# u of batch 2 transposed by TensorE instead of the DMA crossbar, and a new issue order for a fused linear-attention and MLP-mixer kernel

## The chip, the cores and the metric

The kernel runs on one core of a Trainium2 chip. That core has five engines with a queue of instructions each: PE (TensorE, matrix products; its weight loads are shown apart as PEld), DVE (VectorE), ACT (ScalarE), POOL (GpSimd) and SP (SyncE, which here only issues DMA transfers). An engine works through its queue in order, and an instruction that waits for another engine holds up all that stand behind it. The metric is the device time of one execution in microseconds (us). A program reads "faster" or "slower" here only against the same kernel before the change.

## The reference

Four batches, eight heads, 768 positions, head width 48. First a gated linear attention: per head a 48x48 state is decayed by alpha and gets k times v added at each position, and y is q times the state. Then an MLP mixer on x, which is y with the heads side by side (768 positions by 384 columns): one part mixes along the positions (768 to 256 to 768), one along the columns (384 to 1536 to 384).

```python
for t in range(S):
    state = alpha[:, :, t, :, None] * state + np.einsum('bhd,bhe->bhde', k[:, :, t], v[:, :, t])
    y[:, :, t] = np.einsum('bhd,bhde->bhe', q[:, :, t], state)
...
xt = x.transpose(0, 2, 1)
h = np.maximum(xt @ w_tok1, 0.0) @ w_tok2
u = x + h.transpose(0, 2, 1)
h2 = np.maximum(u @ w_ch1, 0.0) @ w_ch2
return (u + h2).astype(np.float32)
```

Inputs and output are float32; the kernel computes most products in bf16.

## The kernel before

The attention is computed in 12 blocks n = 0 to 11: three blocks of 256 positions for each of the four batches, and in a block two halves of 128. Instead of the recurrence the kernel forms logarithms of alpha, sums them along the positions with a triangular product, takes E (the exponential of the sum) and IE (its inverse), scales q by E and k by IE, and then works with plain products and a triangular mask. The mixer of batch b starts when the six x tiles of its three blocks are there, so the attention of later batches is computed between the mixer's products of earlier ones.

There is no scheduler in the kernel. A function `build` makes a list of named steps, each with its tiles and with what has to be done before it. One table of text, `ORDER` (lines 376 to 432), gives the order in which all steps are issued, and with the last letter of each word the engine: t PE, s ACT, v DVE, g POOL, y SP. A second table, `BUFS`, gives the buffer that each new tile takes. So the place of a step among the steps of its engine is what the table says; the waits follow from the tiles. A third rule (`shared`, line 693) makes certain steps on DVE and POOL wait for each other where the table changes from one of the two engines to the other.

The names that matter here, with n a block, b a batch, i one of six row tiles, and half or hf one of two:

- `ld_at`, `ld_kt`, `ld_qt`, `ld_vt` n: loads of alpha, k, q, v (line 548), all issued by SP; `ldw_...`: loads of weights, `cw_...`: their casts to bf16. All of these use 22 buffers named `in`, which the output tiles share.
- `P`, `ln`, `lnP`, `cum`/`cumw`, `E`, `IE` n: the sums and exponentials; `k0a`, `q0r`: products that correct k and q for alternate positions; `kk`, `kl` and `qq`, `ql`: k and q scaled (line 662, tiles `pkk`, `pkq`).
- The scaled k and q have to be transposed. For blocks 0 to 5 PE does it (`trk`, `trq`, line 675, and the evictions `evk`, `evq` to the tiles `tpk`, `tpq`). For blocks 6 to 11 it is done by the DMA crossbar, issued by SP (`dk`, `dq`, line 686, into `tpk`), and `pq` copies the transposed q into `tpq`.
- `G0_`, `G1_`, `mask0_`, `mask1_`: scores and their mask (line 729); `ka`, `kb`, `kc`: halves of the scaled k moved between partitions; `kc` waits for the transpose of k, since it overwrites its source; `K`: products of k and v for the state; `s`, `sa`, `sm`: state; `vb`, `vs0_`, `vs1_`: v cast and moved; `ia`, `ib`, `y0_`, `y1_`: the output products, `x0_`, `x1_`: their eviction.
- Mixer: `t1_b_m_kc` (line 815), `ht_b_m`, `t2_b_i` (line 820), `u_b_i` (line 824). Then u has to be transposed into the tile `ut`, of which there is one buffer. For batches in `UP` PE does it: `up_b_p` for p = 0 to 2 (six transposes of 128x128 each, line 831) and `ut_b_p`, its eviction by DVE or ACT (line 834). For the others the crossbar does it: `ux_b_half` (line 690), two DMAs issued by SP.
- `c1_b_mc_half` (line 839, three products each), `rt_b_mc_half` (lines 810 and 812, eviction with the maximum), `c2_b_i_q` (line 844, three products each), `o_b_i` (line 848), `st_b_i`: store (line 588), issued by SP or ACT.
- `f1_...` and `f3_...`: products of zeros that nobody reads (line 612), 11 steps at the start of the program.

The wait of a step `c1` on the transposed u differs between the two ways:

```python
preds=(uts[0:2 + half] if b in UP else [uts[half]]) + [wl[("wc1", mc // 2)]],
```

With PE, the products of half 0 wait for the first two evictions `ut` and those of half 1 for all three; with the crossbar each half waits for its own DMA.

Of the kernel before, what the change touches and what calls it, by code (L numbers as in the profile page):

```python
# [101 lines left out]
UP = (0, 1)  # L102
# [15 lines left out]
def build(g):  # L118
# [166 lines left out]
    def mixer(b):  # L285
# [27 lines left out]
        uts = []  # L313
        if b in UP:
            for p in range(3):
# [74 lines left out]
rt_0_3_1s cw_wc12g c1_0_5_0t c1_0_6_1t rt_0_6_1s c1_0_0_1t c1_0_1_1t c1_0_4_1t k0a3v kk3v kl3v trk3t kb3s IE4s  # L390
c1_0_5_1t ld_qt3y q0r3v ld_vt3y rt_0_5_0v rt_0_4_1v c1_0_9_0t rt_0_1_1s vb3s vs1_3s vs0_3s ql3g rt_0_7_0v c1_0_2_1t
rt_0_5_1v qq3g trq3t ldw_wc15y cw_wc15s c1_0_8_1t rt_0_0_1v evk3v c1_0_8_0t rt_0_8_0s evq3v rt_0_2_1s rt_0_9_0s ka3g
kc3g K3t s0_3v sa1_3v ld_at5y P5g c1_0_11_0t c1_0_4_0t rt_0_4_0s c1_0_11_1t ld_qt4y q0r4g rt_0_11_0v lnP5s G0_3t ln15s
G1_3t c1_0_10_1t rt_0_11_1s ldw_wc20y c1_0_10_0t cum5t ldw_wc21y rt_0_8_1s mask0_3v mask1_3v rt_0_10_1s c1_0_9_1t
cw_wc20s ld_kt4y ldw_wc22y rt_0_10_0s y0_3t x0_3v IE5s ib3t ldw_wc23y qq4g ql4g trq4t cw_wc21g r15s y1_3t c2_0_4_0t
c2_0_5_0t cw_wc22s c2_0_2_0t c2_0_2_1t evq4v E5s kk4g c2_0_5_1t k0a4v kl4v trk4t sm1_3v evk4v cw_wc23s rt_0_9_1s
c2_0_1_0t ka4g ldw_wc24y x1_3s ld_kt5y k0a5v kk5g kb4g c2_0_1_1t G1_4t mask1_4v cw_wc24s kc4s G0_4t mask0_4v c2_0_5_2t
c2_0_4_1t c2_0_2_2t ldw_wc25y cw_wc25s ld_vt4y vb4s vs0_4s c2_0_4_2t ld_qt5y c2_0_4_3t o_0_4v q0r5v qq5v trk5t
c2_0_1_2t vs1_4s ia4t y0_4t x0_4s t1_1_1_0t t1_1_1_1t evk5s K4t sa0_4v sm0_4g c2_0_5_3t o_0_5v trq5t sa1_4v c2_0_2_3t
o_0_2v c2_0_1_3t t1_1_1_2t ib4t y1_4t evq5s G0_5t mask0_5v ld_at6y P6g sm1_4g G1_5t mask1_5v c2_0_0_0t ld_vt5y  # L400
c2_0_0_1t ld_at7y P7g c2_0_0_2t vb5s vs0_5s kc5s K5t x1_4s c2_0_0_3t ia5t y0_5t t1_1_0_0t t1_1_0_1t c2_0_3_0t sa0_5v
sm0_5v lnP7s lnP6s ld_kt6y k0a6v t1_1_1_3t vs1_5s ib5t y1_5t ld_kt7y k0a7g x0_5s ln16s ld_at8y cum6t P8g t1_1_0_2t
t1_1_0_3t t1_1_0_4t ld_at9y o_0_1v t1_1_1_4t x1_5s t1_1_1_5t o_0_0v ht_1_1v t1_1_0_5t c2_0_3_1t cum7t P9v ld_qt6y r16s
ln17s ht_1_0s t2_1_1t u_1_1v IE6s kk6g t2_1_2t IE7s lnP8s t2_1_0t u_1_0v t2_1_3t u_1_3v ld_qt7y u_1_2v ld_kt8y
c2_0_3_2t ld_vt6y r17s t2_1_4t u_1_4v q0r6g t2_1_5t u_1_5v ld_vt7y up_1_0t up_1_1t ut_1_1v ut_1_0s cum8t E8s c2_0_3_3t
up_1_2t c1_1_0_0t E7s lnP9s dk6y c1_1_11_0t c1_1_1_0t kb6g ld_kt9y q0r7v kk7v rt_1_1_0v E6s c1_1_2_0t rt_1_2_0v
c1_1_6_0t c1_1_5_0t c1_1_9_0t dk7y ut_1_2v c1_1_2_1t rt_1_0_0v c1_1_6_1t rt_1_11_0v o_0_3v rt_1_6_0v rt_1_2_1v qq7g
ld_qt8y vb6s ka6s IE8s rt_1_5_0v qq6g c1_1_7_0t c1_1_4_0t rt_1_4_0v c1_1_3_1t ln18s r18s vs1_6s kc6s vs0_6g K6t s0_6v
rt_1_9_0v rt_1_7_0s k0a9g c2_1_1_0t c1_1_8_0t vb7s vs0_7g c1_1_1_1t sa1_6v ln19s ka7s vs1_7s rt_1_8_0s rt_1_1_1v
c1_1_3_0t rt_1_3_0v k0a8g sm1_6g rt_1_3_1s ld_at10y kk8v P10v c1_1_8_1t dq6y kc7s c1_1_0_1t c1_1_7_1t c1_1_5_1t  # L410
ld_qt10y q0r8v qq8g dq7y rt_1_8_1s c1_1_9_1t c1_1_11_1t kb7s rt_1_5_1v rt_1_7_1s rt_1_6_1s rt_1_0_1v rt_1_9_1v pq6s
c1_1_10_0t lnP10s K7t sa0_7v sm0_7g cum9t IE9s kk9g rt_1_10_0v rt_1_11_1v c1_1_10_1t rt_1_10_1v c1_1_4_1t rt_1_4_1s
c2_1_1_1t c2_1_1_2t sa1_7v sm1_7g ld_vt8y G1_6t mask1_6v G0_6t mask0_6v c2_1_3_0t c2_1_3_1t c2_1_1_3t o_1_1v E9s
# [489 lines left out]
```

## Time and profile before

| | |
|---|---|
| three runs | 162.04, 163.16, 163.5 us; median 163.16 |
| the profiled execution | 162.72 us, of which the span from first to last instruction is 161.0 |
| PE busy | 153.2 us, 95% of the span, 1583 products |
| DVE, ACT, POOL busy | 114.8, 101.7, 68.8 us |
| read from and written to HBM | 25.17 and 4.72 MB |
| granted clock of TensorE | 1.00 |

The span is what the profile explains; 1.7 us of the execution lie outside of it. PE's busy time counts overlapped products once and includes the time in which a product only drains, so it is not a measure of how much could be saved. In the rows of the profile a line of the kernel stands for all steps that use it: line 607 is a helper through which nearly all of the attention's products go, and line 706 and 707 are the copy helper on ACT and on DVE or POOL.

### The profile page before, as it was taken

What the parts mean: (1) busy time and instruction counts of PE and PEld (TensorE: products, weight loads), DVE (VectorE), ACT (ScalarE), POOL (GpSimd) and SP (SyncE); (2) the same over time, 40 slices, a digit from 0 to 9 for tenths busy, and PEclk for the clock granted to TensorE, in tenths of its full rate; (3) what the DMA queues carried; (4) which work ended last, traced back from release to release, by engine and by line L of the source; (5) the groups of instructions that cost most, each with busy time, mean ns of one, the idle gap of its engine ahead of it and who ended that gap; (6) DMA issues with size and microseconds to landing.
All of it is one profiled execution on the core that took longest, in us unless ns stands there. A gap on an engine that the chain in (4) does not pass through costs nothing.

```text
span 161.0 us, 4005 instructions
## 1 busy us (share of the span) xinstructions
PE 153.2 (95%) x1583; PEld 99.3 (62%) x1583; DVE 114.8 (71%) x208; ACT 101.7 (63%) x189; POOL 68.8 (43%) x83
## 2 busy tenths in 40 slices
PE   7988998999999999999999979999999999999992
PEld 4556865556675776766666646666666556666661
DVE  5189996878998898999999849878773632732061
ACT  3789878789997999699998863554832000455000
POOL 4013655217936265789489769991220000000000
PEclk9999999999999999999999999999999999999999
DMA  4999999996999999999999999997402370712035
GB/s 121 325 325 326 360 320 314 333 285 165 337 370 326 246 302 254 269 248 243 182 275 154 216 249 207 222 183 218 151 2 102 62 183 0 274 46 75 0 111 183
DMA packets 76322, 34.46 MB, mean 214 GB/s; under 512 B 68112, under 2 KB 76304, under 8 KB 76304
## 3 DMA queue, kind: packets, MB, share of 16 engines
q1 hardware_dynamic: 74144, 31.27, 76.1%
q10 hardware_dynamic: 2160, 2.95, 5.1%
q8 instruction: 12, 0.20, 0.5%
q14 instruction: 6, 0.05, 0.1%
HBM read 25.17 MB, written 4.72 MB: 186 GB/s over the span
## 4 chain that ended last, share of the span: by engine, by line
PE 87%; DVE 5%; ACT 4%; issue 1%; POOL 0%; DVEq 0%
PE ps L839 29%; PE ps L844 29%; PE ps L607 18%; PE ps L815 5%; PE ps L820 4%; PE ps L675 2%; ACT tpq L706 1%; DVE u L824 1%; DVE pkq L662 1%; DVE pkk L662 1%; PE ps L831 1%; ACT tpk L706 1%; DVE wc L707 1%; ACT IE L646 1%; ACT E L646 1%
## 5 line engine op out<-in xcount | busy, mean ns | idle before, releaser
L844 PE MATMUL ps<-wc,rt 128*128 128x384 bf16 (+2 forms) x300 | 52.7, 319 | 0.0
L839 PE MATMUL ps<-ut,wc 128*128 128x384 bf16 x288 | 50.7, 326 | 0.2
L810 ACT ACTIVATE rt<-ps 128x384 bf16<-128x384 f32 x51 | 23.2, 493 | 27.9 <-PE ps L839 25.2
L839 PEld LDWEIGHTS <-wc 128*128 128x128 bf16 x288 | 27.2, 98 | 17.5 <-DVE wc L707 0.5
L844 PEld LDWEIGHTS <-rt 128*128 128x128 bf16 x300 | 27.3, 98 | 16.3
L812 DVE TENSOR_SCALAR rt<-ps 128x384 bf16<-128x384 f32 x45 | 23.0, 552 | 12.1 <-PE ps L839 11.6
L729 DVE TENSOR_TENSOR gtm<-ps,mk 128x1024 bf16<-128x1024 f32 x24 | 28.5, 1219 | 2.6 <-PE ps L607 2.4
L848 DVE TENSOR_TENSOR in<-ps,u 128x384 f32<-128x384 f32 (+2 forms) x25 | 12.9, 538 | 13.5 <-PE ps L844 13.3
L662 POOL TENSOR_TENSOR pkq<-in,E 128x384 bf16<-128x384 f32 (+1 forms) x12 | 15.7, 1320 | 11.9 <-DVE in L658 5.7
L706 ACT CAST vb<-in 64x384 bf16<-64x384 f32 (+1 forms) x24 | 15.2, 632 | 2.2 <-DMA in<-in_v_dram 0.9
L824 DVE TENSOR_TENSOR u<-ps,x 128x384 bf16<-128x384 f32 x24 | 11.8, 550 | 1.8 <-PE ps L820 1.7
L662 POOL TENSOR_TENSOR pkk<-in,IE 128x768 bf16<-128x768 f32 (+1 forms) x7 | 11.1, 1584 | 3.4 <-DVE pkk L662 1.5
L781 POOL TENSOR_TENSOR ss<-tmp,E 128x384 bf16<-128x384 f32 x9 | 7.5, 833 | 9.7 <-DVE tmp L778 6.5
L706 ACT CAST x<-ps 128x384 bf16<-128x384 f32 x17 | 8.1, 484 | 4.1 <-PE ps L607 3.9
L815 PE MATMUL ps<-x,wt 128*128 128x384 bf16 x48 | 10.5, 326 | 0.0
L820 PE MATMUL ps<-ht,wt 128*128 128x384 bf16 x48 | 9.4, 325 | 0.6 <-ACT ht L810 0.6
L607 PE MATMUL ps<-zs 128*128 128x384 f32 (+1 forms) x22 | 8.5, 517 | 1.1 <-DVE zs L508 1.1
L662 DVE TENSOR_TENSOR pkk<-in,IE 128x384 bf16<-128x384 f32 (+1 forms) x10 | 6.1, 633 | 4.2 <-ACT IE L646 4.0
L707 POOL CAST vb<-in 64x384 bf16<-64x384 f32 (+1 forms) x10 | 5.6, 564 | 7.5 <-PE ps L607 7.0
L607 PE MATMUL ps<-tpq,tpk 48*64 48x128 bf16 (+1 forms) x288 | 8.1, 219 | 0.6 <-ACT tpk L706 0.4
L607 PE MATMUL ps<-vb,gtm 128*128 128x48 bf16 x192 | 8.6, 183 | 0.0
L592 POOL TENSOR_TENSOR in<-in 128x384 f32<-128x384 f32 x7 | 7.0, 1000 | 3.5 <-DMA in<-in_alpha_dram 3.5
(90 smaller groups left out, 208.6 us busy)
## 6 DMA issues: line engine op xcount, KB each, us to landing
in<-in_alpha_dram SPq DMA_DIRECT2D x12, 384.0 KB, 5.6
in<-in_k_dram SPq DMA_DIRECT2D x12, 384.0 KB, 4.9
in<-in_v_dram SPq DMA_DIRECT2D x12, 384.0 KB, 5.2
in<-in_q_dram SPq DMA_DIRECT2D x12, 384.0 KB, 4.9
in<-in_moe_w_ch_dram SPq DMA_DIRECT2D x12, 384.0 KB, 6.0
out_dram<-in ACTq DMA_DIRECT2D x15, 192.0 KB, 1.9
in<-in_moe_w_tok_dram SPq DMA_DIRECT2D x4, 384.0 KB, 6.3
out_dram<-in SPq DMA_DIRECT2D x8, 192.0 KB, 2.1
```

What stands on the lines that cost most here:

```text
L607: return self.pe.matmul(out, lhsT=lhsT, rhs=rhs, start=start, stop=stop, skip_group_check=True)
L662: self.shared(self.eng[e].tensor_tensor(self.t(dst)[:, c : c + z, :, 0:D], self.t(src)[:, :, c : c + z, :].rearrange("p h s d -> p s h d") ...
L706: return self.act.copy(d, s)
L729: self.nc.vector.tensor_tensor(self.t(gtm)[:, hf, :, :], self.pair(gp).rearrange("p a (j t) -> p (a j) t", t=128), bass.AP(tensor=m.tensor ...
L810: self.act.activation(d, s, AF.Relu)
L812: self.nc.vector.tensor_scalar_max(d, s, 0.0)
L815: self.pe.matmul(self.bank(bank)[:, 0:HD], lhsT=self.wt1[:, kc, m * 128 : m * 128 + 128], rhs=self.t(x), start=(kc == 0), stop=(kc == NS - 1))
L820: self.pe.matmul(self.bank(bank)[:, 0:HD], lhsT=self.wt2[:, kc, i * 128 : i * 128 + 128], rhs=self.t(hts[kc]), start=(kc == 0), stop=(kc = ...
L824: self.nc.vector.tensor_tensor(self.t(u)[:, i % 3], self.bank(bank)[:, 0:HD], self.t(x), ALU.add)
L839: self.pe.matmul(self.bank(bank)[:, 0:HD], lhsT=self.wc1[:, kc, mc * 128 : mc * 128 + 128], rhs=self.t(ut)[:, 3 * half : 3 * half + 3, kc, ...
L844: self.pe.matmul(self.bank(bank)[:, 0 : cz - ca], lhsT=self.t(rts[mc][0])[:, i * 128 : i * 128 + 128], rhs=self.wc2[:, mc, ca:cz], start=( ...
L848: self.nc.vector.tensor_tensor(self.row(o)[:, ca:cz], self.bank(bank)[:, 0 : cz - ca], self.t(u)[:, i % 3, ca:cz], ALU.add)
```

## The change

One constant is changed, and the two tables are replaced as a whole (their lines are not shown; a line of each stands for the rest). The number of steps goes from 946 to 950.

```diff
-UP = (0, 1)
+UP = (0, 1, 2)
...
 ORDER = """
-f1_trq1t f3_cumw1t f3_K0t ld_at0y ln0s f3_trk0t ld_at1y ln1s f3_cumw0t cumw0t IE0s cumw1t E1s IE1s Et1s Et0s ld_kt0y
...
+ld_at0y ln0s ld_at1y ln1s f1_trq1t f3_trk0t f3_trq1t f3_cumw0t cumw0t f3_cumw1t ld_qt0y f1_trq0t cumw1t E0s ld_kt0y
...
```

- Batch 2 joins `UP`. The two crossbar DMAs `ux_2_0` and `ux_2_1` go; three steps `up_2_p` with 18 transposes on PE and three evictions `ut_2_p` (two on DVE, one on ACT) come. Batch 3 stays with the crossbar.
- All steps stand in a new order, and some on another engine: 43 instead of 45 of the `rt` evictions on DVE and 53 instead of 51 on ACT; three instead of one of the `pq` on POOL; eight instead of three of the `qq` on DVE; 14 instead of 10 stores on SP. The order is said to have been worked out with the transfers that bring instructions counted as pauses, at places found by counting products; nothing of that stands in the kernel but the table itself.

Three places where the order differs. The first is DVE at the start of the program, blocks 0 to 2, behind the memsets: from the scaled q and k (line 662) to the first masks (`gtm`) and states (`ss`). The tiles: `tpk`, the transposed k; `vb`, the cast v. Before:

```order
L662 TENSOR_TENSOR pkk_97<-in_85,IE_94 128x8x48 x2
L707 CAST vb_102<-in_80 128x768
L772 TENSOR_TENSOR ss_114<-ps,E_90 128x384
L707 COPY tpk_107<-ps 128x1024
L662 TENSOR_TENSOR pkq_95<-in_68,E_90 128x8x48 x2
L662 TENSOR_TENSOR pkq_96<-in_70,E_91 128x8x48 x2
L772 TENSOR_TENSOR ss_115<-ps,E_90 128x384
L662 TENSOR_TENSOR pkk_98<-in_76,IE_93 128x8x48 x2
L729 TENSOR_TENSOR gtm_110<-ps,mk 128x1024 x2
L729 TENSOR_TENSOR gtm_111<-ps,mk 128x1024
L662 TENSOR_TENSOR pkk_99<-in_66,IE_94 128x8x48
```

And in the change:

```order
L662 TENSOR_TENSOR pkq_96<-in_84,E_90 128x8x48 x2
L662 TENSOR_TENSOR pkk_98<-in_77,IE_93 128x8x48 x2
L662 TENSOR_TENSOR pkk_97<-in_64,IE_94 128x8x48 x2
L707 COPY tpk_104<-ps 128x1024
L707 COPY tpk_106<-ps 128x1024
L729 TENSOR_TENSOR gtm_111<-ps,mk 128x1024
L772 TENSOR_TENSOR ss_116<-ps,E_90 128x384
L729 TENSOR_TENSOR gtm_111<-ps,mk 128x1024
L772 TENSOR_TENSOR ss_115<-ps,E_90 128x384
L729 TENSOR_TENSOR gtm_110<-ps,mk 128x1024
L772 TENSOR_TENSOR ss_117<-ps,E_91 128x384
L662 TENSOR_TENSOR pkk_99<-in_69,IE_94 128x8x48 x2
```

The scaled q of block 1 (`qq1`, `ql1`) and the cast `vb0` left DVE, the second transposed k (`evk1`) came to it, the first mask is the ninth instruction of this piece instead of the thirteenth (an x2 is two), and the scalings of block 2, of which one was on DVE before, are all there: two in the last row shown, `ql2` and `qq2` behind it.

The second place is SP's queue in the third quarter of the attention, from the first crossbar transpose (`dk6`) on. `tpk<-pkk` is a `dk`, `tpk<-pkq` a `dq`. Before (`dk6`, `ld_kt9`, `dk7`, `ld_qt8`, `ld_at10`, `dq6`, `ld_qt10`, `dq7`, `ld_vt8`, `ld_qt9`, `dk8`, `dq8`):

```order
L686 DMA_TRANSPOSE tpk_107<-pkk_97 128x8x128
L548 DMA in_81<-in_k_dram 128x8x96
L686 DMA_TRANSPOSE tpk_104<-pkk_98 128x8x128
L548 DMA in_82<-in_q_dram 128x8x96
L548 DMA in_74<-in_alpha_dram 128x8x96
L686 DMA_TRANSPOSE tpk_105<-pkq_96 128x8x128
L548 DMA in_83<-in_q_dram 128x8x96
L686 DMA_TRANSPOSE tpk_106<-pkq_95 128x8x128
L548 DMA in_84<-in_v_dram 128x8x96
L548 DMA in_66<-in_q_dram 128x8x96
L686 DMA_TRANSPOSE tpk_105<-pkk_99 128x8x128
L686 DMA_TRANSPOSE tpk_107<-pkq_96 128x8x128
```

And in the change (`dk6`, `dq6`, `ld_vt9`, `ld_qt8`, `ld_kt9`, `ld_qt9`, `ld_vt8`, `dk7`, `dk8`, `dq7`, `ld_at10`, `dq8`):

```order
L686 DMA_TRANSPOSE tpk_106<-pkk_99 128x8x128
L686 DMA_TRANSPOSE tpk_107<-pkq_95 128x8x128
L548 DMA in_83<-in_v_dram 128x8x96
L548 DMA in_75<-in_q_dram 128x8x96
L548 DMA in_80<-in_k_dram 128x8x96
L548 DMA in_76<-in_q_dram 128x8x96
L548 DMA in_66<-in_v_dram 128x8x96
L686 DMA_TRANSPOSE tpk_107<-pkk_98 128x8x128
L686 DMA_TRANSPOSE tpk_104<-pkk_97 128x8x128
L686 DMA_TRANSPOSE tpk_105<-pkq_96 128x8x128
L548 DMA in_85<-in_alpha_dram 128x8x96
L686 DMA_TRANSPOSE tpk_106<-pkq_95 128x8x128
```

`dq6` moved up to stand behind `dk6`; `dk7` moved down, behind five loads, and `dq7` from the eighth to the tenth of these places.

The third place is DVE around the u of batch 2 (six rows of line 824). Before:

```order
L729 TENSOR_TENSOR gtm_111<-ps,mk 128x1024
L824 TENSOR_TENSOR u_133<-ps,x_119 128x384
L824 TENSOR_TENSOR u_133<-ps,x_123 128x384
L824 TENSOR_TENSOR u_133<-ps,x_118 128x384
L729 TENSOR_TENSOR gtm_111<-ps,mk 128x1024
L707 CAST x_124<-ps 128x384
L824 TENSOR_TENSOR u_130<-ps,x_120 128x384
L824 TENSOR_TENSOR u_130<-ps,x_125 128x384
L824 TENSOR_TENSOR u_130<-ps,x_126 128x384
L729 TENSOR_TENSOR gtm_110<-ps,mk 128x1024 x2
```

And in the change:

```order
L729 TENSOR_TENSOR gtm_111<-ps,mk 128x1024 x2
L824 TENSOR_TENSOR u_132<-ps,x_124 128x384
L824 TENSOR_TENSOR u_131<-ps,x_118 128x384
L824 TENSOR_TENSOR u_131<-ps,x_122 128x384
L824 TENSOR_TENSOR u_131<-ps,x_126 128x384
L824 TENSOR_TENSOR u_132<-ps,x_119 128x384
L824 TENSOR_TENSOR u_132<-ps,x_120 128x384
L707 COPY kt_100<-pkk_97 64x8x48
L707 COPY ut_134<-ps 128x768 x2
L707 CAST x_125<-ps 128x384
```

The six u now stand together, and behind them `ka10` (`kt<-pkk`) stands ahead of the two evictions `ut_2_0` and `ut_2_2`.

130 lines of the change are left out of this document (65 added, 65 removed), and 22 rows, old and new, of the table BUFS.

## Prediction

> **What bounds the kernel now.** I read the page first, then the busy time of a long stretch, then PE's own waits, then the chain that ended last.
>
> ```profile
> span 161.0 us, 4005 instructions
> PE 153.2 (95%) x1583; PEld 99.3 (62%) x1583; DVE 114.8 (71%) x208; ACT 101.7 (63%) x189; POOL 68.8 (43%) x83
> ...
> 31.00:157.80 126.80, 125.69 (x1262) 80.93 (x1262) 91.43 (x155) 77.63 (x150) 57.69 (x60) 1.00 0.78 193
> ```
>
> The second row is the one to dwell on: from 31 us to the last product PE is busy for 125.69 of 126.80 us at full clock. Only 1.11 us of that long part is idle. So PE bounds the kernel, and what a new order could win behind 31 us is 1.1 us at most; the rest could only come from the start and from the 3.2 us behind the last product.
>
> ```profile
> PE ps L607 <- DVE zs L508: 1.1, 1, 1.1
> PE ps L607 <- POOL pkk L707: 1.1, 1, 1.1
> PE ps L820 <- ACT ht L810: 0.6, 1, 0.6
> PE ps L607 <- ACT la L601: 0.5, 1, 0.5
> ```
>
> PE's waits name nearly all of it: the start, one wait for `pkk` on POOL, and two in the first 31 us. The chain shows what that start consists of:
>
> ```profile
> 6.70 0.82 ACT IE L646
> 7.54 1.03 DVE pkk L662 x2
> ...
> 12.71 1.20 ACT tpq L706
> 13.96 1.21 ACT tpq L706
> 15.17 0.88 ACT tpk L706
> 16.10 1.87 PE ps L607 x45
> ...
> 25.67 0.50 ACT ht L810
> ...
> 30.08 0.87 DVE wc L707
> 30.99 6.02 PE ps L839 x36
> ...
> 157.56 0.33 issue
> ```
>
> Three evictions in a row on ACT (`evq0`, `evq1`, `evk1`) hold up PE until 16.1, `ht` holds it at 25.7, and the cast of a weight (`cw_wc11`) until 30.99. From there it is products to the end.
>
> **The change part by part.** *Eighteen transposes more on PE.* Their price stands in batch 1:
>
> ```profile
> 37.02 0.45 PE ps L675 x8
> ...
> 65.87 0.67 PE ps L831 x12
> ...
> L831 PE MATMUL ps<-idn,u 128*128 128x128 bf16 x36 | 2.9, 220 | 0.1
> ...
> L707 DVE COPY ut<-ps 128x768 bf16<-128x768 bf16 x4 | 2.2, 548 | 0.0
> L706 ACT COPY ut<-ps 128x768 bf16<-128x768 bf16 x2 | 1.6, 788 | 1.5 <-PE ps L831 1.5
> ```
>
> Twelve in 0.67 are 0.056 us each, so 18 cost 1.0 us, all of it on the path, since PE has no idle time to hide them: **+1.0**. The three evictions (two of 0.55 on DVE, one of 0.79 on ACT) need cover. Behind `up_2_0` PE still has `y0_9`, `up_2_2` and `c2_1_2_3` to do, 8, 6 and 3 products or 0.20 + 0.34 + 0.49 = 1.03 us by their steps in the trace; an eviction on DVE with the latency of a product (about 0.2) takes 0.75. It is covered if DVE is free then, which is a rival below.
>
> The Trainium skill (VectorE: DVE Perf Modes, The three transpose paths) gives 390 ns for a 128x128 bf16 transpose by TensorE and 1309 ns by the crossbar. If each of the 18 held PE for that long, the estimate from that page would be 7.0 us instead of 1.0. The row of twelve in 0.67 us speaks against reading the figure so: it is a latency, and the transposes overlap.
>
> *Two crossbar DMAs less.*
>
> ```profile
> DMA to landing us min/median/max: 3.3/3.4/5.8
> ```
>
> That is from issue to landing for the four `ut` DMAs, and nothing is named as waiting for them: PE had `c2_1` products and an attention block in between. Taking the first two out wins nothing on PE. If their cover had been gone it would have been up to 3.4; a gain here is excluded, because PE was not idle there.
>
> *The wait of `K9`.*
>
> ```profile
> 86.86 2.66 SPq L686 DMA_TRANSPOSE tpk<-pkk  x1
> ...
> DMA to landing us min/median/max: 3.0/4.8/6.7
> ...
> 93.69 0.50 POOL L707 COPY pkk<-pkk 64x384 bf16<-64x384 bf16 x1 [1.81 <-ACT x L706]
> ...
> 94.25 0.34 PE L607 MATMUL ps<-vb,pkk 128*128 128x96 bf16 x4 [1.06 <-POOL pkk L707]
> ```
>
> `kc9` on POOL is named as released by ACT, but by the code it waits for `dk9`, and `dk9` issued at 86.86 with the longest landing of its kind (6.7) arrives at 93.56, just ahead of 93.69. In the change `dk9` has two loads fewer in front of it and `K9` 1.9 us more PE work, so I take the wait as gone: **-1.06** (ends: 0 and -1.06).
>
> *The start.*
>
> ```profile
> 4.32 0.84 ACT L601 ACTIVATE la<-in 128x768 bf16<-128x768 f32 x1 [2.23 <-DMA in<-in_alpha_dram]
> ...
> 103.26 2.36 DVE L729 TENSOR_TENSOR gtm<-ps,mk 128x1024 bf16<-128x1024 f32 x2 [0.65 <-PE ps L607]
> ```
>
> Before, the first scores wait for `evq0` (12.71 + 1.20 = 13.9), and the first mask comes at about 14.5. In the change `E0` and `qq0`, `ql0` go first, and `evk0`, `evk1` are on DVE. With the same loads (`alpha` of blocks 0 and 1, then q, k) I add: `ln0` ends at 5.16, so the sum of block 0 starts at 5.2 and lasts 1.0; `E0` 0.82 (as `IE0`) to 7.1, two scalings 1.03 to 8.1, `trq0` to 9.1, `evq0` on ACT behind the exponentials of block 1 from 9.6 to 10.9, scores to 11.6; an estimate from these rows. From there to `ht_0_1` DVE has 6 masks at 1.17 (half of 2.36) and 12 instructions at 0.47 (two in a row take 1.03, the last of them 0.56), together 12.7, and three waits of 0.2 to 0.5 (for `K0`, `G0_1`, `y1_2`), an estimate of 1.0 in all: 25.3, against 25.5 before. So the 2.9 us won on the first mask are given back, since three scalings came from POOL to DVE. Next, `cw_wc12` on DVE stands in the place of `cw_wc11`, behind `ut_0_1`, and the second `c1` starts at 31.0 as before. But `trk3` (0.45) is then already done on PE, where it came at 36.9 before: **-0.4** (ends: -1.5, if DVE's waits fall away and the weight comes earlier; +1.0, if block 2's v comes late).
>
> *Everything else that moved.* Before, there is 0.05 us of unexplained idle time behind 31 us, so it can only get worse. Where it is tight is shown by the queue of SP:
>
> ```profile
> 5.51 2.34 SPq L548 DMA_DIRECT2D in<-in_q_dram  x2
> ...
> 80.49 2.60 SPq L686 DMA_TRANSPOSE tpk<-pkk  x1
> 83.20 1.24 SPq L686 DMA_TRANSPOSE tpk<-pkq  x1
> ...
> 85.06 0.64 PE L607 MATMUL ps<-tpq,tpk 48*64 48x128 bf16 x32
> ```
>
> Loads in a row go at 1.17 each; a transpose behind a load takes 2.6, behind a transpose 1.24. In the change five loads stand between `dq6` and `dk7`, and `dq7` is the third transpose behind them. `dq6` waits for `qq6` on DVE, which ends at about 70.4: before, 75.4 us of PE's work, by the counts of its products, were done when `G0_7` began at 85.06, so the offset is 9.7, less the 0.4 of the start; `qq6` stands at 60.1 us of work, and takes 0.96. Then 1.24 + 5 x 1.17 + 2.6 + 1.24 + 1.24 later the issue of `dq7` is done (82.6), and it lands some 2.0 to 4.2 behind that (the landing row above counts 3.0 to 6.7 from the start of an issue of 1.24 to 2.6): 84.6 to 86.8. `pq7` takes 1.35, and PE reaches `G0_7`, with 77.7 us of work ahead of it, at 77.7 + 9.3 = 87.0. So the wait lies between 0 and 1.2. A second such place follows on POOL (below). I take **+0.6** for all of these, near the lower end (ends: 0 and 3), since the loads and transposes of 65 to 111 us run at the pace of the queue either way and a wait at one place gives slack at the next. Bringing instructions, 12 transfers of 16 KB for PE, stays the same in number within one, and no wait of PE's products is put down to it; I set it at nothing.
>
> Sum against the profiled execution: 162.72 + 1.0 - 1.06 - 0.4 + 0.6 = 162.86. That execution was 0.44 below the median of the three runs; I go a third of that way up and forecast **163.0**.
>
> **The rivals.** *The transposed q and k come late (slower).* Blocks 7 to 9 depend in the change on one another: `dk9` is written into the buffer that `pq7` reads, so it can't be issued before `pq7` ends, and `dq9` stands behind it. `pq9` went to POOL, and there the work of block 10 follows in a row:
>
> ```profile
> 94.61 1.34 ACT L706 COPY tpq<-tpk 128x1024 bf16<-128x1024 bf16 x1 [0.90 <-DMA tpk<-pkq]
> ...
> 102.72 0.64 PE L607 MATMUL ps<-tpq,tpk 48*64 48x128 bf16 x32
> ...
> L707 POOL COPY tpq<-tpk 128x1024 bf16<-128x1024 bf16 x1 | 1.3, 1345 | 0.1
> L662 POOL TENSOR_TENSOR pkq<-in,E 128x768 bf16<-128x768 f32 x6 | 10.1, 1682 | 3.9 <-DVE in L658 2.0 <-DVE pkk L662 1.7
> L781 POOL TENSOR_TENSOR ss<-tmp,E 128x384 bf16<-128x384 f32 x9 | 7.5, 833 | 9.7 <-DVE tmp L778 6.5 <-ACT tpq L706 3.1
> L654 POOL TENSOR_TENSOR in<-in,in 128x384 f32<-128x384 f32 x5 | 5.0, 999 | 2.8 <-DVE in L654 2.6
> L662 POOL TENSOR_TENSOR pkk<-in,IE 128x768 bf16<-128x768 f32 x5 | 9.1, 1816 | 1.9 <-DVE in L654 0.9 <-ACT IE L641 0.8
> ```
>
> `pq9`, `qq10`, `sm1_9`, `P11`, `k0a10`, `kk10` are 1.35 + 1.68 + 0.83 + 1.0 + 1.0 + 1.82 = 7.7 us. Behind `kk10` waits `ka10` on DVE, and behind that the two evictions `ut_2_0` and `ut_2_2`, without which no `c1_2` can start. `c1_2_0_0` has 93.1 us of PE's work ahead of it; `G0_10`, with 91.1, began at 102.72 before, so without the 1.06 and the 0.4 it is due at 103.2. So `kk10` has to end by 102.2 (0.27 for `ka10`, 0.55 and the latency for the eviction) and `dq9` to land by 94.5. It landed at 94.6 before, where `pq9` was released. From there on each us of delay is a us on PE, for which nothing else stands ready. If the queue is 2 to 3 us later than I reckon, the time is 164.8 to 166.0. Against it: fewer loads lie ahead of `dk9`, and neighbouring transposes are cheap. Chance 0.28.
>
> *The start gives more (faster).* If the early mask isn't given back, because DVE's other instructions find gaps, `ht_0_0` and u come up to 1.5 earlier beyond my 0.4: 161.3 or a little below. Against it: by the counts DVE has three scalings more to do there now, and the casts of weights behind it wait for loads that land no earlier. Chance 0.10.
>
> *Each transpose holds PE for its whole latency.* By the row above a product of this form lasts 0.22 when alone; 18 in line would be 4.0, not 1.0, and the time 166.0. The page of the Trainium skill named above would make it 169.0. The row of twelve speaks against both. Chance 0.02.
>
> *The forecast*, PE full with a few small waits: 0.60.
>
> **How the numbers follow.** 1%, 1.6 us, is about what a measurement of this kernel can tell from no change. The forecast's own range is 161.8 to 164.6: inside. The late transposes and the serial ones lie beyond it above (0.30), the better start below (0.10). The range that should hold 8 in 10 takes in half of either side: 161.4 to 165.5.
>
> **What would show it.** In the profile after: `L831` with 54 products; PE busy some 1.0 us longer and its idle time behind 31 us below 1.1 us; no wait of `K9`; the first mask near 11.6 and the second `c1` still near 31. It is wrong if PE waits at `G0_7`, `G0_9` or the first `c1_2` for more than 1 us together, or if the weights' products start more than 1 us away from 31.

## The result and the profile after

| | before | after |
|---|---|---|
| median, on the same chip | 162.37 us | 163.43 us |
| lowest to highest | 161.49 to 163.5 | 162.72 to 163.85 |
| after / before | | 1.0057, 95% interval 1.0039 to 1.0076 |
| the profiled execution | 162.72 us | 162.93 us |

The change makes the kernel slower by 0.6%, about 0.9 us by the ratio and 1.06 by the two medians. (The ratios are worked out from the fast runs on each chip and can differ a little from the quotient of two medians.) The forecast was 163.0, inside 1% of no change. Against its own base, the profiled execution, it allowed the change 0.14 us; beside the median of 163.16 shown for before it was even a small gain, of 0.16. So the time was 0.43 off, but a loss of about 1 us was forecast as a draw. The two profiled executions alone, 0.2 us apart, would have confirmed the forecast: most of what follows is about why that would have been wrong.

The page of the kernel after, its first and its busy line, and the busy time from 31 us to 158 us (columns: length, then busy time and instructions of PE, PEld, DVE, ACT, POOL, then granted clock, DMA share, GB/s):

```profile
span 161.2 us, 4044 instructions
PE 154.4 (96%) x1601; PEld 100.3 (62%) x1601; DVE 119.2 (74%) x214; ACT 98.1 (61%) x184; POOL 66.7 (41%) x85
```

```profile
31.00:158.00 127.00, 126.88 (x1275) 81.76 (x1273) 95.33 (x160) 75.53 (x149) 53.33 (x59) 1.00 0.75 190
```

PE has 18 products more, and is idle for 0.12 us in 127. The bound is what it was; there is simply more in it. PE's waits in the kernel after:

```profile
PE ps L607 <- DVE zs L508: 1.1, 1, 1.1
PE ps L820 <- ACT ht L810: 0.6, 1, 0.6
PE ps L607 <- DVE gtm L729: 0.4, 1, 0.4
PE ps L675 <- DVE pkk L662: 0.3, 1, 0.3
PE ps L815 <- DVE x L707: 0.3, 1, 0.3
```

All five lie in the start. The wait for `pkk` on POOL (`K9`) is gone, as forecast. The chain that ended last, up to the row of `c1` products:

```profile
4.26 5.05 DMA in<-in_k_dram
9.40 1.03 DVE pkk L662 x2
11.09 2.14 PE ps L607 x35
...
28.81 1.20 DVE u L824 x3
30.75 0.87 DVE wc L707
31.67 5.05 PE ps L839 x30
```

The three evictions on ACT that stood in the chain of before are out of it; loads and DVE took their place, and the long row of `c1` stands in it from 31.67 on instead of 30.99.

To compare more than two executions I split each profile at one point: the first product of the second `c1` step (the 30.99 and 31.67 of the two chains), and the end of the last product. What lies behind that end is 4.81 to 4.88 us in the profiled executions of before and after, and plays no part. All figures are read or subtracted from the traces; the kernels are told of below. A wait is counted here from the moment at which the product would have followed the one before it; the rows of the profile count idle time from the end of that product, and show 0.16 to 0.19 us less for the same wait.

| kernel | second c1 at | last product ends | between | wait of PE over 0.3 us in between |
|---|---|---|---|---|
| before | 30.99 | 157.84 | 126.85 | 1.22 at `K9` |
| before, copy (b_copy) | 31.83 | 157.70 | 125.87 | none |
| before, copy (b_copy2) | 31.84 | 159.08 | 127.24 | 1.36 in block 5 (0.80 at a `c2_0`, 0.56 at `trk5`) |
| before, copy (b_copy3) | 31.93 | 158.28 | 126.35 | none |
| e3, `dk9` earlier | 31.21 | 156.87 | 125.66 | none |
| e8, `dk9` later | 31.00 | 157.26 | 126.27 | 0.61 at `c1_2_1_0` |
| e5, PE transposes in the old order | 32.30 | 159.94 | 127.63 | 0.74 at `G0_10` |
| after | 31.67 | 158.12 | 126.45 | none |
| after, copy (a_copy) | 31.52 | 157.95 | 126.43 | none |
| e6, transposes twice | 32.47 | 159.89 | 127.42 | none |
| e11, three transposes | 31.54 | 157.96 | 126.42 | three of 0.2 to 0.3, 0.76 together |

### The profile page after: what moved, and what is told of

Read it like the earlier page. It is cut to its first block, busy times and chain, and to the rows that moved or that the text cites. A ratio compares the mean times of both kernels' runs of the same rounds, so it can differ in the third digit from the quotient of the medians.

```text
span 161.2 us, 4044 instructions
## 1 busy us (share of the span) xinstructions
PE 154.4 (96%) x1601; PEld 100.3 (62%) x1601; DVE 119.2 (74%) x214; ACT 98.1 (61%) x184; POOL 66.7 (41%) x85
## 4 chain that ended last, share of the span: by engine, by line
PE 84%; DVE 6%; DMA 3%; SPq 2%; ACT 1%; issue 1%; POOL 1%; DVEq 0%; POOLq 0%
PE ps L844 29%; PE ps L839 29%; PE ps L607 14%; PE ps L815 5%; PE ps L820 4%; DMA in<-in_k_dram 3%; SPq L548 2%; DVE u L824 1%; PE ps L675 1%; PE ps L831 1%; DVE pkk L662 1%; DVE ss L772 1%; DVE pkq L662 1%; DVE wc L707 1%; POOL vb L707 1%
## 5 line engine op out<-in xcount | busy, mean ns | idle before, releaser
L844 PE MATMUL ps<-wc,rt 128*128 128x384 bf16 (+2 forms) x300 | 51.9, 320 | 0.0
L839 PE MATMUL ps<-ut,wc 128*128 128x384 bf16 x288 | 49.9, 326 | 0.1
L810 ACT ACTIVATE rt<-ps 128x384 bf16<-128x384 f32 x53 | 24.2, 492 | 22.6 <-PE ps L839 22.3
L662 POOL TENSOR_TENSOR pkk<-in,IE 128x384 bf16<-128x384 f32 (+1 forms) x8 | 11.2, 1407 | 7.6 <-DVE in L654 5.7
L707 POOL CAST vb<-in 64x384 bf16<-64x384 f32 (+1 forms) x15 | 8.5, 569 | 11.5 <-DVE pkq L662 3.7
L706 ACT CAST vb<-in 64x384 bf16<-64x384 f32 (+1 forms) x18 | 11.8, 656 | 1.6 <-DMA in<-in_v_dram 0.9
L662 POOL TENSOR_TENSOR pkq<-in,E 128x384 bf16<-128x384 f32 (+1 forms) x7 | 8.1, 1167 | 9.5 <-DMA in<-in_q_dram 7.9
L781 POOL TENSOR_TENSOR ss<-tmp,E 128x384 bf16<-128x384 f32 x8 | 6.7, 837 | 10.5 <-DVE pkq L662 8.5
L662 DVE TENSOR_TENSOR pkq<-in,E 128x384 bf16<-128x384 f32 (+1 forms) x10 | 7.4, 755 | 4.5 <-ACT E L646 3.5
L592 POOL TENSOR_TENSOR in<-in 128x384 f32<-128x384 f32 x8 | 8.0, 1003 | 0.4 <-DMA in<-in_alpha_dram 0.2
```

What stands on the lines that cost most here:

```text
L662: self.shared(self.eng[e].tensor_tensor(self.t(dst)[:, c : c + z, :, 0:D], self.t(src)[:, :, c : c + z, :].rearrange("p h s d -> p s h d") ...
L706: return self.act.copy(d, s)
L810: self.act.activation(d, s, AF.Relu)
L839: self.pe.matmul(self.bank(bank)[:, 0:HD], lhsT=self.wc1[:, kc, mc * 128 : mc * 128 + 128], rhs=self.t(ut)[:, 3 * half : 3 * half + 3, kc, ...
L844: self.pe.matmul(self.bank(bank)[:, 0 : cz - ca], lhsT=self.t(rts[mc][0])[:, i * 128 : i * 128 + 128], rhs=self.wc2[:, mc, ca:cz], start=( ...
```

## The experiments

In the diffs of this section that move a step, the table `ORDER` is written with one word on a line; `BUFS` changes with it and is not shown.

**The kernels unchanged, once more.** Two copies of before and after, and later two more of before.

> The kernel before, unchanged, for a second profile. Theory A (the wait of K9 is a fixed part of the order): PE again waits 1.0 to 1.1 us ahead of K9, and about 1.1 us of idle time behind 31 us. Theory B (the wait depends on when the crossbar transpose dk9 lands, which differs between executions): the wait ahead of K9 differs by 0.4 us or more, and the span with it.

> The changed kernel, unchanged, for a second profile; its first one was 0.5 us below its median. Theory A: the same 0.1 us of idle time behind 31 us, and a longer start. Theory B: some place of the stretch from 85 to 104 us (G0_7, G0_8, G0_9, K9 or the first c1_2) has a wait of 0.3 us or more that the first profile does not show.

> The kernel before unchanged, for one more profile of it. Of the profiles with its order in the middle so far, one (the first, with dk9 landing 6.7 us behind the start of its issue) has a wait of K9. If that wait is rare, none here, with dk9 landing 3.5 to 4.5 behind its issue; if it is there about half of the time, as likely as not.

> As the run before it: the kernel before unchanged, for one more profile of where dk9 lands, whether K9 waits, and when the second c1 begins (30.99 to 32.30 so far).

Measured 162.54 (b_copy), 162.78 (a_copy), 163.92 and 163.12 us (b_copy2, b_copy3), one execution each, beside a median of before of 162.59 and 162.24 on those chips. None of the three copies of before has the wait of `K9`. In b_copy POOL's copy `kc9` runs at 92.17 without any wait (in the first profile: at 93.69, behind a wait of 1.81), and PE has 0.55 us of idle time in 127 (0.30 of it behind its last product) instead of 1.11 in 126.8. POOL's row, and the busy time:

```profile
92.17 0.50 POOL L707 COPY pkk<-pkk 64x384 bf16<-64x384 bf16 x1
```

```profile
31.00:158.00 127.00, 126.45 (x1266) 81.17 (x1265) 92.57 (x157) 77.79 (x152) 57.80 (x60) 1.00 0.77 195
```

But b_copy2 has a loss of the same kind at another place, where only b_copy3 has a trace of it (0.27): in block 5, PE waits for a cast of a weight and for a scaled k.

```profile
53.90 0.49 PE L844 MATMUL ps<-wc,rt 128*128 128x384 bf16 x2 [0.64 <-ACT wc L706]
54.78 0.62 PE L675 MATMUL ps<-idn,pkk 128*128 128x128 bf16 x8 [0.39 <-POOL pkk L662]
```

So single waits of about 1 us come and go in before, at places that differ from one execution to the next. The two profiles of the kernel after differ by 0.02 us between the second `c1` and the end; the longer start that was expected of a_copy did not come (31.52).

**The wait of K9: dk9 issued earlier, and later.**

```diff
 ...
+dk9y
 ld_kt10y
-dk9y
 ...
```

> Before, with the crossbar transpose dk9 issued one place earlier, ahead of the load of k of block 10. Theory A (a wait of 1.06 us ahead of K9 in each execution): ratio 0.9935, and no wait at K9 in the profile. Theory B (the wait is there in some executions only, and smaller in the median): ratio 0.996 to 1.000.

Ratio to before 0.9992 (0.9955 to 1.0029), median 162.24. There is no wait of `K9` in the profile, and nothing clear is won: in us the interval reaches from -0.7 to +0.5, so that a wait of 1.06 in every execution (ratio 0.9935) is excluded. The other direction:

```diff
 ...
+dq9y
 dk9y
 ...
-dq9y
 ...
```

> The kernel before, with the transposing DMA dq9 issued ahead of dk9 instead of behind it; nothing else is moved. dk9 then lands one transpose later, at 93.4 to 94.6 us, where PE is ready for K9 at about 93. Theory B (K9 waits for dk9 alone, and what it waits goes into the time in full): a wait of K9 of 1.0 to 2.4 us in the profile, and a time 0.7 to 1.8 us above before, ratio 1.004 to 1.011. If a wait at K9 is given back later (PE has waits of 0.2 us only behind it, so there is little to give it back from), ratio at most 1.002.

Ratio 1.0004 (0.9969 to 1.004): missed. I had expected that `dk9` lands where `dq9` did. SP's queue and POOL's `kc9` in e8:

```profile
86.67 1.40 SPq L686 DMA_TRANSPOSE tpk<-pkq  x1
88.17 1.26 SPq L686 DMA_TRANSPOSE tpk<-pkk  x1
```

```profile
92.39 0.51 POOL L707 COPY pkk<-pkk 64x384 bf16<-64x384 bf16 x1 [0.96 <-DMA tpk<-pkk]
```

Though issued second, `dk9` landed at 92.27, 4.1 us behind the start of its issue, and PE, which reached `K9` at 93.0, did not wait. Behind its issue it landed 4.3 us in b_copy, 5.5 in b_copy2, 4.3 in b_copy3, 4.5 in e3, 3.2 in after, and 6.7 in the first profile of before, the one on which the prediction was built. So e8 did not make `dk9` late, and its time says nothing of what a late one costs. That the `K9` wait goes into the time in full where it occurs is not shown by these runs, since none of them made it occur.

**The price of the transposes in the old order.** Before, with batch 2 in `UP`; first with all three evictions on ACT.

```diff
-UP = (0, 1)
+UP = (0, 1, 2)
...
 c2_1_5_1t
+up_2_2t
+ut_2_2s
 ...
 c2_1_5_2t
+up_2_0t
+ut_2_0s
 c2_1_5_3t
+up_2_1t
+ut_2_1s
-ux_2_1y
 ...
-ux_2_0y
```

> Before, with batch 2 of u transposed by PE and nothing else moved: the two crossbar DMAs out, three PE steps and three evictions on ACT in. If 18 transposes cost 0.056 us each on the path: 1.0 us slower than before, ratio 1.006. If the crossbar DMAs that are gone make room in the queue that PE feels: ratio 1.000 to 1.003. If each transpose holds PE for its latency of 0.22 us: 4 us slower, ratio 1.024.

Ratio 1.0242 (1.0196 to 1.0288), which is about the 4 us that a price of 0.22 for each transpose would give. The trace says otherwise. PE's waits between 80 and 110 us in e1, and one row of its time line:

```profile
PE ps L607 <- ACT ut L706: 1.1, 2, 0.8
PE ps L607 <- ACT la L598: 0.8, 1, 0.8
```

```profile
103.25 0.33 PE L607 MATMUL ps<-la,u 128*128 128x400 bf16 x1 [0.78 <-ACT la L598]
104.00 0.50 PE L831 MATMUL ps<-idn,u 128*128 128x128 bf16 x6
104.34 0.65 PE L844 MATMUL ps<-wc,rt 128*128 128x384 bf16 x3
```

Six transposes take 0.34 us until the next step begins; but the evictions hold up ACT's logarithm for `cum11`, and PE waits. A number that agreed with a wrong theory by accident: the placing of the evictions cost more than the transposes. The second trial places them where DVE and ACT have room:

```diff
 y1_9t
+up_2_2t
 ...
 x1_9s
+ut_2_2s
 ...
 c2_1_5_2t
+up_2_0t
+ut_2_0v
 c2_1_5_3t
+up_2_1t
+ut_2_1v
 ...
```

> The kernel before, with only batch 2 transposed by PE: up_2_2 behind y1_9, up_2_0 and up_2_1 on both sides of c2_1_5_3, their evictions on ACT (ut_2_2, behind x1_9) and DVE (the two others, behind u_2_2), the two crossbar DMAs gone. Unlike the first trial of this edit, no eviction stands behind a row of ACT's logarithms, and up_2_1 writes into a PSUM bank that was read long before. Theory C (the price of the 18 transposes, 1.0 us, is what is left of the change, and the two DMAs taken out win nothing): 1.0 to 1.2 us slower than before, ratio 1.006 to 1.008, three steps of L831 of about 0.34 us each more, and at most 0.3 us of new waits near 100 to 105 us. Theory D (the transposes are hidden or nearly free, and what the change lost, it lost by its order): ratio 0.998 to 1.002. If each transpose held PE for 0.22 us: 4.0 us, ratio 1.024.

Ratio 1.0134 (1.0106 to 1.0162), 2.2 us. PE in e5, time line:

```profile
101.30 0.49 PE L831 MATMUL ps<-idn,u 128*128 128x128 bf16 x6
...
103.60 0.50 PE L831 MATMUL ps<-idn,u 128*128 128x128 bf16 x6
104.03 0.24 PE L607 MATMUL ps<-tpq,tpk 48*64 48x128 bf16 x1
104.82 0.64 PE L607 MATMUL ps<-tpq,tpk 48*64 48x128 bf16 x31 [0.55 <-DVE ut L707]
```

The second product of `G0_10` waits 0.74 us for a PSUM bank that `ut_2_1` is still reading. Between the second `c1` and the end e5 has 127.63, less that wait 126.89: 1.0 to 1.2 above the undisturbed 125.66 and 125.87. So theory C's size is met in the trace, but the time by itself is 1 us above what C allowed: 0.74 of it is the wait. The profile also began late (32.30), which a profile of one execution cannot attribute.

**The price in the new order, upward and downward.**

```diff
-                self.pe.transpose(o[:, c : c + 128], self.t(u)[:, (2 * p + q) % 3, j * 128 : j * 128 + 128], self.idn)
+                for _ in range(n):
+                    self.pe.transpose(o[:, c : c + 128], self.t(u)[:, (2 * p + q) % 3, j * 128 : j * 128 + 128], self.idn)
```

Here n is 2 for batch 2 and 1 for the others.

> The kernel after, in which each of the 18 transposes of batch 2 is issued twice into the same place (the result stays the same): 18 products more, no DMA, no eviction and no other instruction more. It measures their price by itself. Theory C: 1.0 us above the kernel after, so 1.9 to 2.1 above before, ratio 1.012 to 1.013; the three steps of up_2 take 0.67 us instead of 0.34. Theory D: within 0.3 us of the kernel after, ratio 1.005 to 1.008. At 0.22 us for each: 4.0 above after, ratio 1.030.

Ratio 1.0124 (1.0097 to 1.0152), 1.1 us above the kernel after. PE in after, and in e6:

```profile
102.14 0.83 PE L831 MATMUL ps<-idn,u 128*128 128x128 bf16 x12
102.81 0.36 PE L607 MATMUL ps<-vb,gtm 128*128 128x48 bf16 x8
103.01 0.49 PE L831 MATMUL ps<-idn,u 128*128 128x128 bf16 x6
103.34 0.65 PE L844 MATMUL ps<-wc,rt 128*128 128x384 bf16 x3
```

```profile
102.95 1.50 PE L832 MATMUL ps<-idn,u 128*128 128x128 bf16 x24
104.28 0.36 PE L607 MATMUL ps<-vb,gtm 128*128 128x48 bf16 x8
104.49 0.83 PE L832 MATMUL ps<-idn,u 128*128 128x128 bf16 x12
```

From one start to the next, 12 transposes take 0.67 and 24 take 1.33; between the second `c1` and the end e6 has 127.42 against 126.45. That is 0.97 us for 18, 0.054 each: the predicted price. Now downward, with 15 of the 18 left out:

```diff
-                self.pe.transpose(o[:, c : c + 128], self.t(u)[:, (2 * p + q) % 3, j * 128 : j * 128 + 128], self.idn)
+                if n or q + j == 0:
+                    self.pe.transpose(o[:, c : c + 128], self.t(u)[:, (2 * p + q) % 3, j * 128 : j * 128 + 128], self.idn)
...
-                  self.bank(bank).bitcast(BF16)[:, 0:768])
+                  bass.AP(tensor=z.tensor, offset=z.offset, ap=[list(z.ap[0]), [0, 6], [1, 128]]))
```

Here n is false for batch 2, and z is the first 128 columns of the bank.

> The kernel after, with 15 of the 18 transposes of batch 2 left out: each step of up_2 does its first only, and the evictions copy that one block six times over, so batch 2's result is not the reference's; order, evictions, DMAs and everything else stay. With the run that doubles them it shows whether the price is the same downwards. Theory C (all of the change's loss is the price of these products): 0.75 to 0.85 us below the kernel after, so within 0.3 of before, ratio 1.000 to 1.003. If something else of the new order (an eviction, a queue, the start) stands just behind them: less than 0.4 below after, ratio 1.003 to 1.006.

Ratio 1.0063 (1.0038 to 1.0089): no gain at all, where theory C expected 0.8; it is what was expected if something stands just behind the transposes. PE in e11 at this place, and DVE:

```profile
102.00 0.27 PE L832 MATMUL ps<-idn,u 128*128 128x128 bf16 x2
102.40 0.36 PE L607 MATMUL ps<-vb,gtm 128*128 128x48 bf16 x8
102.86 0.22 PE L832 MATMUL ps<-idn,u 128*128 128x128 bf16 x1
102.92 0.65 PE L849 MATMUL ps<-wc,rt 128*128 128x384 bf16 x3
103.62 2.12 PE L844 MATMUL ps<-ut,wc 128*128 128x384 bf16 x12
```

```profile
99.94 2.87 DVE L824 TENSOR_TENSOR u<-ps,x 128x384 bf16<-128x384 f32 x6
102.84 0.26 DVE L707 COPY kt<-pkk 64x384 bf16<-64x384 bf16 x1
103.02 1.01 DVE L707 COPY ut<-ps 128x768 bf16<-128x768 bf16 x2
```

PE has holes in front of `y0_9`, `up_2_2` and the first `c1_2`, 0.76 us together: the six u in a row on DVE, and the evictions behind them, set the pace. The busy time from 99 to 105 us, in after and in e11, says the same: DVE is full in both, and PE is full in after only because the transposes fill it.

```profile
99.00:105.00 6.00, 6.00 (x68) 4.10 (x67) 5.94 (x13) 3.38 (x7) 3.27 (x3) 1.00 1.16 257
```

```profile
99.00:105.00 6.00, 5.71 (x53) 3.40 (x52) 5.94 (x12) 3.50 (x8) 3.11 (x3) 1.00 1.01 270
```

From the second `c1` to the last product e11 takes 126.42 us and after 126.45. So theory C was too simple. In the new order PE and DVE are both full in this stretch: more products cost their full price, fewer of them win nothing.

**The order alone.** After, with the crossbar for batch 2.

```diff
-UP = (0, 1, 2)
+UP = (0, 1)
...
 u_2_1v
+ux_2_0y
 ...
 u_2_5v
+ux_2_1y
```

(The six steps `up_2` and `ut_2` are gone.)

> The kernel after in its own order, with batch 2's u transposed by the crossbar as before: up_2 and ut_2 are gone, ux_2_0 is issued behind u_2_1, and ux_2_1 behind u_2_5, ahead of dq10. It does the order alone. Theory C: 1.0 us of PE's work goes, and in its place PE waits at the first c1_2 products, since in this order only c2_1_2_2, t2_2_5, cum11, y1_9, y0_9 and c2_1_2_3 (2.0 us) stand between the last u of the first half and c1_2_0_0, against 3.4 us or more of a crossbar DMA: a wait of 1.4 to 2.0 for the first half and 0.3 to 1.0 for the second. Together 0.7 to 2.0 above the kernel after, ratio to before 1.010 to 1.019. Theory D (the order alone is what costs): 1.004 to 1.008. If the DMAs were covered: ratio 0.998 to 1.002.

Ratio 1.0413 (1.0371 to 1.0455), some 5.5 us above after: far beyond the expected 0.7 to 2.0. In e9, SP's queue, PE's time line, and the busy time in stretches:

```profile
103.07 3.31 SPq L690 DMA_TRANSPOSE ut<-u  x2
```

```profile
103.76 0.65 PE L844 MATMUL ps<-wc,rt 128*128 128x384 bf16 x3
107.69 6.58 PE L839 MATMUL ps<-ut,wc 128*128 128x384 bf16 x23 [3.28 <-DMA ut<-u]
```

```profile
103.00:108.00 5.00, 1.47 (x26) 0.76 (x22) 3.67 (x8) 2.70 (x6) 0.35 (x1) 0.83 0.83 156
108.00:113.00 5.00, 5.00 (x17) 2.37 (x16) 0.30 (x1) 0.49 (x1) 1.33 (x1) 0.50 1.03 267
```

The first DMA landed 4.6 us behind its issue instead of 3.4, so PE stood for 3.28 us; and behind that its granted clock was 0.50 for about five us, in which the steps of `c1` took 0.96 us instead of 0.49. The wait cost its length and then some 2.7 us more. The Trainium skill (TensorE: Matmul & The Clock Gate, What's actually happening) says that the clock is halved after an idle window of about 3.4 us and restored after a busy one of that length. The trace agrees in kind; here a wait of 3.28 us was enough, and the half clock lasted longer than 3.4 us. For this experiment it means that it does not measure the order alone. It does show that with the two DMAs at these places this order has no cover for them: they need PE's transposes, or other places.

**The start.** After, with three edits ahead of 32 us.

```diff
+y1_2t
 t1_0_1_2t
-y1_2t
 ...
-k0a3v
 ht_0_1v
 ...
+k0a3g
 kk3g
 ...
+c1_0_11_0t
 c1_0_5_0t
```

> The kernel after, with three edits in its start: y1_2 on PE ahead of t1_0_1_2, the scaling k0a3 on POOL ahead of kk3 instead of on DVE ahead of ht_0_1, and c1_0_11_0 (whose weight is there already) ahead of c1_0_5_0, which waits for the cast cw_wc12. If the start of the change is late by the order of DVE's and PE's own work (theory C: 0.2 to 0.3 us at x1_2 and 0.28 at the second c1), PE reaches the row of c1 products with 0.3 to 0.5 us less idle time, and all of it reaches the end: 0.3 to 0.5 below the kernel after, ratio to before 1.002 to 1.004. If the start goes at the pace of the loads, which land at the same times, nothing is won: 1.005 to 1.007.

Ratio 1.0044 (1.0022 to 1.0067), against 1.0057 for after. The intervals overlap: inconclusive, though on the side of a small gain.

The start of after, joined to the rest of before at the first `c2_0`:

```diff
-f1_trq1t
-f3_cumw1t
...
+ld_at0y
+ln0s
...
 c2_0_4_0t
 c2_0_5_0t
...
```

> The order of the kernel after on every engine and queue up to the first c2_0 (about 48 us), then that of the kernel before for all that is left; batch 2 by the crossbar, as before. It does the start's part of the change alone, trk3 and trk4 ahead of their old places included. The prediction's step (-0.4): ratio 0.996 to 0.999. If the start gains nothing in the median, since PE's late filler, the loads and DVE give back what the early mask wins: 0.999 to 1.002. If it costs (the second c1 began at 31.5 to 31.7 in the profiles of the kernel after, at 31.0 to 32.3 in those with the start of before, and the work done ahead is only 0.45): 1.002 to 1.005. At the seam a few waits of 0.2 to 0.3 us near 48 to 52 us are possible, which belong to neither order and are taken off by the trace.

Ratio 1.0355 (1.0306 to 1.0403). The seam spoiled it. The longest of PE's waits in e12:

```profile
PE ps L607 <- ACT la L598: 2.8, 1, 2.8
```

It is `cum5`, from 46.9 to 49.7 us, whose logarithm stands late in the joined order; another wait of 1.2 us follows at 62.2. The time therefore tells nothing of the start; its trace only adds one more beginning of the row of `c1` with this start, 32.58.

The last experiment came out of the rows of the first products. PE's first row, products of zeros which nobody reads, in before, in b_copy, in e5 and in after:

```profile
1.12 4.70 PE L607 MATMUL ps<-zs 128*128 128x128 f32 x10 [1.12 <-DVE zs L508]
```

```profile
1.12 5.61 PE L607 MATMUL ps<-zs 128*128 128x128 f32 x10 [1.12 <-DVE zs L508]
```

```profile
1.12 5.91 PE L607 MATMUL ps<-zs 128*128 128x128 f32 x10 [1.12 <-DVE zs L508]
```

```profile
1.12 4.04 PE L607 MATMUL ps<-zs 128*128 128x128 f32 x8 [1.12 <-DVE zs L508]
```

Before, b_copy and e5 have the same ten products there, in the same order, and they take 4.70, 5.61 or 5.91 us; `cumw0` stands behind them. In the eight profiles with this start `cumw0` begins at 5.59 to 6.83, and the second `c1` follows 25.3 to 25.9 us behind it: most of what differs between their starts is there from these first products on. So I left two of them out:

```diff
-f3_cumw0t
 cumw0t
 ...
 c1_0_0_0t
+c1_0_1_0t
 c1_0_3_0t
 ...
-c1_0_1_0t
 ...
+dk9y
 ld_kt10y
-dk9y
```

> The kernel before with three edits, none of them on batch 2: the filler products f3_cumw0 (on zeros, which no one reads) are left out ahead of cumw0, c1_0_1_0 (whose weight is there) stands ahead of c1_0_3_0, which waits for the cast cw_wc11, and dk9 is issued ahead of the load ld_kt10. In the traces so far the same ten filler products of before last 4.70 to 5.91 us, and cumw0 starts behind them at 5.66 to 6.83, though ln0 ends at 5.16. If the start of before is set by these fillers, cumw0 starts at 5.2 to 5.6, the row of c1 products begins 0.4 to 1.0 earlier, and the time is 0.4 to 1.2 below before, ratio 0.993 to 0.998. If DVE and the loads set the start at 20 to 30 us, only the 0.28 at c1_0_3_0 is won: ratio 0.998 to 1.000. If the filler is needed to bring PE up to speed, the products behind it are slower for longer: ratio 1.000 to 1.004.

Ratio 0.9979 (0.9959 to 1.0), median 161.77 against 162.24; in the profile `cumw0` begins at 5.32 and the second `c1` step at 30.71, the earliest of all. The row of `c1` itself begins at 30.23, no earlier than in the first profile of before (30.22), whose filler was short. The ratio lies on the border of two expectations, and the run does not tell the three edits apart. It is the fastest kernel of this study: it beats the kernel after, and leads before by 0.2%, an interval that just touches no difference.

## Why the prediction was right or wrong, by its steps

- **What bounds the kernel: right.** PE is full from 31 us on in both kernels.
- **Eighteen transposes, +1.0: right in size.** 0.97 by e6. The rival in which each holds PE for its latency is refuted: the rows count 0.22 us for one alone, and 12 in a row take 0.67. The Trainium skill (TensorE: Matmul & The Clock Gate, Wait — 56ns, not 53.3ns?) gives 55.6 ns from start to start for a product of 128 columns, which is what the rows show; so of its two pages it is this one, not the 390 ns of the transpose paths, that prices such a row. What the prediction did not see is e11: DVE is as full as PE there, so it is not the transposes alone that hold this stretch.
- **Two crossbar DMAs less, nothing won: right**, with a remark: e8's 0.61 us at `c1_2_1_0` is a wait for one of them, and b_copy and b_copy3 wait 0.2 us for the other, so their cover is thin in some executions.
- **The wait of K9, -1.06: this is the step that failed.** The reading of the wait was right (it is `dk9`, not ACT), and it is indeed absent after the change. For the two profiled executions the whole sum even holds: PE's last product comes 0.28 us later (158.12 against 157.84), by +0.97 for the transposes, -1.22 for `K9`, +0.23 for the start (0.68 later, less the 0.45 of `trk3`) and about +0.3 for the rest, and 0.14 was forecast. But the wait was taken as a fixed part of before. It occurs in one of the four profiles of the kernel before, and moving `dk9` forward (e3) changes the time by -0.1 us, with an interval of -0.7 to +0.5. Against the median of before the term is about -0.1, not -1.06. That the forecast's base was only 0.35 us above the median in spite of this wait comes from its start: 30.99, where three of its four profiles began their second `c1` at 31.83 to 31.93. A lucky start and an unlucky landing, and the prediction wrote off only the second.
- **The start, -0.4: mis-sized, about 0.** The first mask came at 11.81, as forecast (11.6). But `ht_0_1`, forecast for 25.3, came at 26.0: `y1_2` stands behind a product that it need not wait for, and `k0a3` (0.5 us of DVE) stands ahead of `ht_0_1`. Eight profiles with the start of before (the seven of the table above that have it, and e1 with 31.82) began the second `c1` at 31.6 on average (30.99 to 32.30), six with that of after (after, a_copy, e6, e9, e11, e12) at 32.1 (31.52 to 32.69): +0.5, against the 0.45 of `trk3`, which is done ahead. With spreads as large as these the 0 is uncertain by several tenths, and e7, which mends the two places, is inconclusive.
- **Everything else, +0.6: too much.** The waits at `G0_7` and `G0_8` are 0.15 and 0.11 us. The rival of the late q and k missed by a little: `dq9` landed at 94.10, where the prediction had put the limit at 94.5, and nothing waited.

The sum with measured terms: +0.97, -0.1, 0 and about +0.3 make about +1.2; measured were 0.9 to 1.1. As a check, take the averages of the second `c1` (31.6 and 32.1) and 4.85 behind the last product. After comes to 163.4 with its 126.4 us in between, for a median of 163.43. Before comes to 162.2 if nothing waits in between (125.7), and to 162.8 with the average of the six profiles of its order with the crossbar (126.4), for a median of 162.37.

What stays open is what a median execution of either kernel looks like, since none was profiled. The four profiles of before (162.54 to 163.92 us) all lie above its median of 162.37 (b_copy, 162.54, is level with the 162.59 of its own chip), and the two of after (162.93 and 162.78) lie below its median of 163.43; by the last products of these six (158.2 on average before, 158.0 after) the change would lose nothing. So the runs show the price of the transposes and that `K9` is no fixed term. That the start and the order come to nothing is worked out from traces with large spreads; the two experiments that were to show it by the time (e9, e12) brought waits of their own, so it is not shown by itself.

## What to carry to other kernels

A wait in one profile is a term of the sum only if it is there in a second profile of the same kernel; look at two or three before booking the gain of removing it, and look also for what was lucky in that execution. Where PE and DVE are both full in a stretch, price a change there in both directions: adding work costs in full, and removing it may win nothing as long as the other engine stays full. When a trial's time agrees with a theory, read the row it is about before believing it (e1 did so by accident).

## What the hardware showed that was not expected

- **PE's slow first microseconds are of varying length.** The same ten products of zeros took 4.63 to 5.91 us, depending on the execution: a step of two of them takes 1.28 us at first and 0.64 later, and the moment of the change differs. The column of the granted clock doesn't show it: in e5 it reads 1.00 in a stretch in which the steps still took 1.28. (The trace's own record of the clock begins only at 7.25 us in e5, and at 4.46 in before; ahead of that the column has nothing to go by.)

```profile
5.00:6.00 1.00, 1.00 (x3) 0.58 (x2) 0.00 (x0) 0.65 (x2) 0.00 (x0) 1.00 1.17 325
```

  The Trainium skill (TensorE: Matmul & The Clock Gate, What you observe) puts the doubling of the rate at about 4 us of sustained products, within 0.5 from run to run. That it varies agrees, but the 1.3 us between the shortest and the longest row is more than the 1.0 which that allows.

  These 1.3 us are as much as the whole effect of this change.
- **Behind a wait of 3.28 us the clock was halved** for about five us (0.50 in the row of e9 above), so that the wait cost nearly twice its length. Behind the 2.8 us of e12's profile it stayed at 1.00.
- **One crossbar DMA lands at very different times.** `dk9` landed 3.1 to 6.7 us behind the start of its issue over the kernels; in the unchanged kernel before alone, with the same neighbours in the queue, it was 4.3, 4.3, 5.5 and 6.7. In the order of the change, where SP issues nothing in the two us ahead of it, it was 3.14 to 3.17 in all six profiles (after, a_copy, e6, e7, e9, e11). That the free queue is the reason was not tested.
